# A planner's transfer costs and a second PSUM bank for the last projections, in a fused attention and two-layer-pair kernel

## The chip, the core and the metric

The kernel runs on one core of a Trainium2 chip. The core has five engines that each work through their own instructions in order: TensorE (PE in the profile; its weight loads are a row of their own, PEld), VectorE (DVE), ScalarE (ACT), GpSimd (POOL) and SyncE (SP), which here only issues DMA transfers. The metric is the device time of one execution in microseconds (us); the median of some runs is compared.

## What is computed

```python
def _attn_ref(q, k, v):                       # q, k, v: 8 x 8 heads x 576 x 64
    k_p = k.reshape(B, H, Sp, pool, D).mean(axis=3)      # pool = 8, Sp = 72
    v_p = v.reshape(B, H, Sp, pool, D).mean(axis=3)
    scores = scale * np.matmul(q, k_p.transpose(0, 1, 3, 2))
    attn = np.exp(scores - max); attn = attn / (sum + 1e-09)
    return np.matmul(attn, v_p)
...
def _moe_ref(x, w_in, w_out, g_ln):           # x: 4608 x 512, d_ff 1024
    h = x @ w_in
    solu = h * softmax(h)
    ln = (solu - mu) / np.sqrt(var + 1e-06) * g_ln
    return ln @ w_out
...
def _moe2_ref(x, w_in, w_out):                # d_ff 2048
    h = x @ w_in
    return (h / (1.0 + np.exp(-1.702 * h))) @ w_out
```

The output of each part is the input of the next. The weights come as 8-byte floats and are joined to one number on the chip.

## The kernel before

The kernel has two parts. The **first part** (the first 539 us) computes attention and the first pair of layers and prepares all weights. It works on 36 tiles of 128 tokens. For tile t the steps are, with the names of the program:

- `attention(t)`: load `qt`; PE makes the scores in the PSUM tile `psx`; DVE takes their maximum (`mx`) and subtracts it into `e` (or ACT does it in eight exponentials); ACT takes the exponential; DVE sums (`rs`), ACT and DVE invert the sum; POOL or DVE multiplies; ACT and POOL split the result into two 2-byte halves `st`; SP issues a transposing DMA from `st` to `aT`; PE multiplies `aT` with the values `vst` into the PSUM tile `psv`; ACT and DVE split that into `xT`.
- `Pair.hidden(j)`: PE multiplies `xT` with `w1i` into `psh` (24 products of 512 columns); DVE, ACT and DVE again work on it (`hmx`, `nm`, `he`, `tt`, `mean`, `vs`).
- `Pair.norm()`, for two tiles together: ten small POOL instructions (`q`, `v`, `r`, `a`, `mean`), then for each of the two tiles ACT (`tt`, `zs`), POOL (`zs`) and a transposing DMA to one half of `zT`.
- `Pair.project(half)`, two halves for each of the 18 pairs: 48 products of 256 columns of `zT` with `w1o` into the PSUM tile `psy`; ACT copies `psy` to `y` (two buffers); SP stores `y` to `y_dram`.

Beside that, 16 chunks of the weights of the second pair of layers are loaded (`raw`), joined, combined and split (`w_f`, `hi`, `lo`) by ACT, DVE and POOL, and stored to `w2i_dram` and `w2o_dram`. When the last of them is done, `prepare_second` reloads the seven tiles `w2i` (1 MB each), loads the first block of tokens `y` in four transfers, measures it (`yam`, a diagonal `diag0`, one product into `psx`), scales and splits it into `ys`.

What order these steps take on each engine is set by `Plan.run` while the program is built: a list scheduler. Every step has modelled costs; among the steps that could come next it takes the one with the least of modelled start time and pulled due time, and appends its instruction to its engine's queue. `Op` costs of transfers come from the helper `D` (lines 502 to 507). `take` lets transfers pass one after the other through a modelled resource "dma". The engines then run their queues in that order, whatever the real times are.

PSUM has eight banks here: `psh` twice two, `psx` two, `psy` one, `psv` one. Since `psy` is one tile with one buffer, the second half of a projection may start only when ACT has copied out the first.

The **second part** takes 12 blocks of 384 tokens through the second pair of layers, with the banks `bank_a`, `bank_b` and `bank_d`, in an order that is written out by hand; the change doesn't touch it. Its first instruction on ACT writes the tile `c`, in memory that the first part's `y` buffers held, so it waits for the last store of `y`.

```python
def D(dst, src, turn=False, short=1):
    ...
    n = math.prod(dst.shape) * mybir.dt.size(dst.dtype)
    return Op(("sp",), emit, [dst], [src], {"sp": n / 360 * (1.23 if turn else short)}, turn)
```

Of the kernel before, what the change touches and what calls it, by code (L numbers as in the profile page):

```python
# [8 lines left out]
F32 = mybir.dt.float32  # L9
# [9 lines left out]
P = 128  # L19
B, H, S, D = 8, 8, 576, 64  # L20
# [5 lines left out]
DM = H * D  # L26
# [6 lines left out]
YB = 2 * P  # L33
# [138 lines left out]
class Plan:  # L172
# [30 lines left out]
    def drop(self, *tiles):  # L203
        for t in tiles:
            del self.ring_of[t.name]
# [75 lines left out]
def moe_kernel(ctx: ExitStack, tc: tile.TileContext, qT, kT, vT, w_in, w_out, g_ln, w2_in, w2_out, eye, outT):  # L281
# [135 lines left out]
    with ExitStack() as ph:  # L417
# [7 lines left out]
        psy = ph.enter_context(tc.tile_pool(name="psy", bufs=1, space=PSUM))  # L425
        psv = ph.enter_context(tc.tile_pool(name="psv", bufs=1, space=PSUM))
# [9 lines left out]
        start, drop = plan.start, plan.drop  # L436
# [4 lines left out]
        def there(*ins):  # L441

            return Op(("none",), lambda engine: None, [], ins, {"none": 0})
# [55 lines left out]
        def A(**kw):  # L499
            return op(("act",), "activation", (), kw)  # L500

        def D(dst, src, turn=False, short=1):
            def emit(engine):
                (nc.sync.dma_start_transpose if turn else nc.sync.dma_start)(dst, src)

            n = math.prod(dst.shape) * mybir.dt.size(dst.dtype)
            return Op(("sp",), emit, [dst], [src], {"sp": n / 360 * (1.23 if turn else short)}, turn)

        def T(products):
            def emit(engine):  # L510
                for p in products:
                    nc.tensor.matmul(*p[:3], start=p[3], stop=p[4])  # L512

            outs, ins = {}, {}
            for p in products:
                outs[str(p[0].offset)] = p[0]
                for x in p[1:3]:
                    ins[x.name, x.offset] = x
            c = sum(
                (count(p[2]) * 0.417 + 3 if p[2].dtype == F16 else count(p[2]) * 1.667 + 6)  # L520
                * (0.5 if count(p[1]) == P // 2 else 1)
                for p in products
            )
            return Op(("pe",), emit, list(outs.values()), list(ins.values()), {"pe": c})
# [86 lines left out]
        def raw_load(raw, src, i, n, q):  # L611
            return D(
                raw.rearrange("p q f t -> p q (f t)"),
                src[i * q * P : (i + 1) * q * P, :].bitcast(I32).rearrange("(q p) f -> p q f", p=P),
            )
# [73 lines left out]
        def g_scale():  # L689
            yield D(g_col, g_ln.rearrange("(k p) -> p k", p=P))  # L690
            am, alln = s1("gam"), s1("galln")
            yield absmax_op(am, g_col)
            yield from largest(am, alln, TINY)
            yield from power_scale("_g", alln, 1.0, g_up, g_dn)
            yield V("tensor_scalar_mul", g_col, g_col, g_up)
# [62 lines left out]
        def half(kind, b, j, src, dst):  # L758

            raw = yield New(kv, [P, 2, SP, NPOOL], F32, "half", bufs=3)  # L760
            begun[kind][b] += 1
            yield D(raw.rearrange("p a s o -> p a (s o)"), src[b][:, 2 * j : 2 * j + 2])
            yield from total(G if KV_POOL.get((kind, b)) == j else V, dst[:, 2 * j : 2 * j + 2], raw)
            drop(raw)
# [138 lines left out]
        class Pair:  # L903
# [91 lines left out]
            def project(self, half):  # L995

                yield there(self.zT, *w1o)
                ps = yield New(psy, [P, 2, YB], F32, "psy", "psy")
                for q in range(2):
                    m = 2 * half + q  # L1000
                    yield T(
                        [
                            (
                                ps[:, q],
                                w1o[w][:, k, m * P : (m + 1) * P],
                                self.zT[:, i * K1 + k, :],
                                k == 0 and w == 0 and i == 0,
                                k == K1 - 1 and w == 1,
                            )
                            for k in range(K1)  # L1010
                            for w, i in PASSES
                        ]
                    )
                y = yield New(sb, [P, 2, YB], F32, "y", bufs=2)
                yield A(out=y, in_=ps, func=AF.Copy)
                drop(ps)
                i, o = divmod(self.i * YB, YD)
                yield D(y_dram[i][:, 2 * half : 2 * half + 2, o : o + YB], y)
                drop(y)
# [144 lines left out]
        q_loaded, scored, turned, valued, hid = ([False] * NTILE for _ in range(5))  # L1164
# [315 lines left out]
```

## Time and profile before

| | |
|---|---|
| three runs | 1255.22, 1255.65 and 1250.54 us; median 1255.22 us |
| the profiled execution | 1253.29 us, span from first to last instruction 1251.5 us |
| PE matmul, busy | 1143.5 us, 91% of the span |
| PE weight loads, busy | 989.6 us, 79% |
| ACT, DVE, POOL, busy | 766.5, 730.9, 664.7 us (61, 58, 53%) |
| projections (`psy`) | 1728 matmuls, mean 273 ns as the profile gives them |
| `hidden` (`psh`) | 864 matmuls, mean 389 ns |
| DMA | 152.85 MB, mean 122 GB/s |

The busy shares are means over two parts that differ: in the first all engines and the DMA work together, in the second PE alone is close to full. A matmul's listed duration includes the time that it overlaps the next one, so that 48 projection matmuls take 5.40 us and not 48 times 273 ns. What the engines wait for is read from the timeline and from the list of waits, for one stretch at a time.

### The profile page before, as it was taken

The page shows a single profiled execution, that of the slowest core. Times are in us where ns is not written, and L with a number is a line of the kernel's source. Part 1 is how long each engine was busy: PE and PEld are TensorE (multiplying, and loading weights), DVE is VectorE, ACT ScalarE, POOL GpSimd, SP SyncE. Part 2 cuts the span into 40 slices and gives each one's busy share as a digit, 9 for nine tenths or more (in the row PEclk, how much of TensorE's full clock was granted, in tenths as well). Part 3 has the DMA queues.
Part 4 walks back from the last instruction along what each step waited for, and adds up shares of the span by engine and source line. Part 5 has one row for each costly group of instructions (what it writes and reads, how often), then busy time and mean ns, then how long its engine had stood idle before and what let it go on. Part 6 is the DMA issues. An engine that isn't in the chain of part 4 may idle for free.

```text
span 1251.5 us, 27586 instructions
## 1 busy us (share of the span) xinstructions
PE 1143.5 (91%) x11678; PEld 989.6 (79%) x11678; DVE 730.9 (58%) x1153; ACT 766.5 (61%) x1073; POOL 664.7 (53%) x696
## 2 busy tenths in 40 slices
PE   2778998899999999889999999999999999999998
PEld 2335665576666666789999999999999898999998
DVE  7898877587677843136455454637272737364543
ACT  6998998788789855345445353627263536454552
POOL 5887998687879953424333352525262515243331
PEclk9989999899999999999999999999999999999999
DMA  9979999999989698470101010100011010101000
GB/s 324 302 205 240 269 270 256 248 231 248 256 206 234 164 230 236 109 270 8 46 14 39 14 40 20 33 27 27 27 33 46 7 46 8 46 7 46 14 14 26
DMA packets 246524, 152.85 MB, mean 122 GB/s; under 512 B 163584, under 2 KB 226176, under 8 KB 244096
## 3 DMA queue, kind: packets, MB, share of 16 engines
q1 hardware_dynamic: 246400, 151.09, 45.5%
q8 instruction: 91, 1.49, 0.5%
q14 instruction: 33, 0.27, 0.1%
HBM read 77.66 MB, written 33.55 MB: 89 GB/s over the span
## 4 chain that ended last, share of the span: by engine, by line
PE 30%; POOL 12%; DVE 8%; ACT 8%; issue 5%; DMA 0%; ACTq 0%; POOLq 0%
PE bank_a L1290 18%; PE bank_d L1290 8%; ACT w_g L1325 6%; DVE g L1337 5%; POOL w_g L336 3%; PE bank_b L1290 3%; POOL w_g L335 3%; POOL w_g L333 2%; POOL w_g L334 2%; PE psy L512 2%; ACT g L1334 1%; DVE c L1303 1%; POOL zs L475 1%; DVE w_g L333 0%; ACT c L1300 0%
## 5 line engine op out<-in xcount | busy, mean ns | idle before, releaser
L1290 PEld LDWEIGHTS <-w2i 128*128 128x128 f16 x4032 | 337.4, 98 | 34.3 <-issue 33.7
L1290 PEld LDWEIGHTS <-w2o 128*128 128x128 f16 x4032 | 335.0, 98 | 7.4 <-issue 6.8
L333 POOL TENSOR_TENSOR w_g<-w_g 128x384 f32<-128x384 f32 x36 | 43.6, 1211 | 379.3 <-ACT w_g L1325 379.3
L1290 PE MATMUL bank_a<-ys,w2i 128*128 128x192 f16 x2304 | 215.1, 247 | 27.1 <-ACT c L1300 25.0
L512 PE MATMUL psh<-w1i,xT 128*128 128x512 f16 x864 | 205.8, 389 | 8.9 <-DVE mean L475 8.2
L1290 PE MATMUL bank_a<-g,w2o 128*128 128x192 f16 x2304 | 206.0, 246 | 1.0
L512 PE MATMUL psy<-zT,w1o 128*128 128x256 f16 x1728 | 196.8, 273 | 8.8 <-ACT y L475 8.8
L512 PEld LDWEIGHTS <-w1o 128*128 128x128 f16 x1728 | 167.9, 98 | 35.8 <-issue 10.3
L1337 DVE SCALAR_TENSOR_TENSOR g<-w_g,gu_b,g 128x1152 f16<-128x1152 f32 (+1 forms) x96 | 169.1, 1782 | 24.5 <-ACT g L1334 24.4
L512 PEld LDWEIGHTS <-xT 128*128 128x128 f16 x864 | 84.4, 100 | 103.9 <-issue 13.8
L1300 ACT ACTIVATE c<-bank_a 128x384 f32<-128x384 f32 x192 | 91.7, 484 | 116.4 <-PE bank_a L1290 113.1
L1334 ACT ACTIVATE g<-w_g,gu_b 128x1152 f16<-128x1152 f32 (+1 forms) x96 | 132.9, 1408 | 39.4 <-POOL w_g L336 39.0
L1303 DVE SCALAR_TENSOR_TENSOR c<-bank_d,c 128x384 f32<-128x384 f32 x96 | 53.3, 555 | 134.4 <-ACT c L1300 99.5
L475 POOL TENSOR_TENSOR zs<-tt,zs 128x1024 f16<-128x1024 f32 x36 | 77.4, 2149 | 59.7 <-ACT zs L475 59.5
L1290 PE MATMUL bank_d<-ys,w2i 128*128 128x192 f16 x1152 | 107.5, 249 | 0.3 <-DVE c L1303 0.3
L1290 PE MATMUL bank_d<-g,w2o 128*128 128x192 f16 x1152 | 102.4, 246 | 3.0 <-DVE g L1337 3.0
L1325 ACT ACTIVATE w_g<-c,ch_b 128x1536 f32<-128x1536 f32 x48 | 75.3, 1568 | 36.8 <-DVE c L1303 36.7
L1300 ACT ACTIVATE c<-bank_a,co_b 128x384 f32<-128x384 f32 x47 | 26.9, 573 | 108.6 <-PE bank_a L1290 108.6
L512 PE MATMUL psx<-kbd,qt 128*128 128x144 f32 (+1 forms) x320 | 46.3, 306 | 24.6 <-ACT raw_z L475 12.7
L512 PEld LDWEIGHTS psx<-kbd,qt 128*128 128x128 f32 (+1 forms) x320 | 41.4, 193 | 29.4 <-issue 12.7
L475 POOL TENSOR_TENSOR lo<-w_f,hi 128x512 f16<-128x512 f32 (+1 forms) x46 | 62.2, 1365 | 2.7 <-ACT hi L475 2.3
L475 DVE TENSOR_REDUCE hmx<-psh 128x1 f32<-128x1024 f32 x36 | 43.7, 1214 | 34.1 <-PE psh L512 34.1
(189 smaller groups left out, 1693.1 us busy)
## 6 DMA issues: line engine op xcount, KB each, us to landing
raw<-w_out SPq DMA_DIRECT2D x12, 1024.0 KB, 6.9
raw<-w_in SPq DMA_DIRECT2D x10, 1024.0 KB, 8.0
half<-kT SPq DMA_DIRECT2D x16, 576.0 KB, 5.4
half<-vT SPq DMA_DIRECT2D x16, 576.0 KB, 5.5
qt<-qT SPq DMA_DIRECT2D x36, 256.0 KB, 3.9
y_dram<-y SPq DMA_DIRECT2D x36, 256.0 KB, 2.8
y<-y_dram SPq DMA_DIRECT2D x48, 192.0 KB, 3.2
outT<-c SPq DMA_DIRECT2D x48, 192.0 KB, 1.9
```

Source lines behind the costliest of these rows:

```text
L333: eng.tensor_tensor(out=w[:, 1], in0=q[:, Q12], in1=q[:, Q11], op=ALU.subtract)
L334: eng.tensor_tensor(out=w[:, 2], in0=q[:, Q22], in1=w[:, 1], op=ALU.subtract)
L335: eng.tensor_tensor(out=w[:, 0], in0=q[:, Q22], in1=q[:, Q12], op=ALU.subtract)
L336: eng.tensor_tensor(out=w[:, 3], in0=q[:, Q21], in1=w[:, 2], op=ALU.subtract)
L475: getattr(eng, name)(*args, **kw)
L512: nc.tensor.matmul(*p[:3], start=p[3], stop=p[4])
L1290: nc.tensor.matmul(bank[:, q], self.weight(p, q, kk, w), self.data(p, kk, i), start=(first and q == 0 and kk == 0 and w == 0 and i == 0), ...
L1300: nc.scalar.activation(out=self.c[:, i], in_=bank, func=AF.Copy, scale=self.scale)
L1303: nc.vector.scalar_tensor_tensor(out=self.c[:, i], in0=bank, scalar=self.scale, in1=self.c[:, i], op0=ALU.mult, op1=ALU.add)
L1325: nc.scalar.activation(out=self.w[:, 0:4], in_=self.c, func=AF.Gelu_apprx_sigmoid, scale=self.ch)
L1334: nc.scalar.activation(out=self.g[:, 0, s], in_=self.w[:, s], func=AF.Copy, scale=self.gu)
L1337: nc.vector.scalar_tensor_tensor(out=self.g[:, 1, s], in0=self.w[:, s], scalar=self.gu, in1=self.g[:, 0, s], op0=ALU.mult, op1=ALU.subtract,)
```

## The change

Two edits, both in the first part.

```diff
-        def D(dst, src, turn=False, short=1):
+        def D(dst, src, turn=False):
...
-            return Op(("sp",), emit, [dst], [src], {"sp": n / 360 * (1.23 if turn else short)}, turn)
+            return Op(("sp",), emit, [dst], [src], {"sp": n / (170 if turn else 330)}, turn)
...
             def project(self, half):
...
-                ps = yield New(psy, [P, 2, YB], F32, "psy", "psy")
+                if half and valued[-1]:
+                    flat = yield New(psv, [P, DM], F32, "psv", "psv")
+                    ps = flat.rearrange("p (a t) -> p a t", a=2)
+                else:
+                    flat = ps = yield New(psy, [P, 2, YB], F32, "psy", "psy")
...
-                drop(ps)
+                drop(flat)
```

The first changes the modelled time of every transfer: a plain one of n bytes is counted n/330 ns in place of n/360, and a transposing one n/170 in place of n/293 (360/1.23). For the 512 KB of an `aT` or a `zT` half that is 3.08 us in place of 1.79. No instruction's work changes by that; the planner's order does, on every engine, from the start of the first part to its end. The second lets the second half of a projection go to the bank `psv` once the planner has placed the values' product of the last tile (`valued[-1]`). In the built program that holds for the last four pairs: four of the 36 projection halves go to `psv`.

**Values and hidden layer of a tile.** PE, at tile 32 of 36, before: the end of that tile's product with the values (`psv_5478`), and what follows; `xT_5168` is tile 30.

```order
5021 L512 MATMUL psv_5478<-aT_5263,vst1_120 64x128
5022 L512 LDWEIGHTS vst1_120
5023 L512 MATMUL psv_5478<-aT_5263,vst1_120 64x128
5024 L512 LDWEIGHTS xT_5168
5025 L512 MATMUL psh_5345<-w1i0_115,xT_5168 128x512
```

PE at the same tile, after: `psv_5606` is tile 32's product with the values, and `xT_5623` is made from it.

```order
5201 L512 MATMUL psv_5606<-aT_5528,vst1_120 64x128
5202 L512 LDWEIGHTS vst1_120
5203 L512 MATMUL psv_5606<-aT_5528,vst1_120 64x128
5204 L512 LDWEIGHTS xT_5623
5205 L512 MATMUL psh_5643<-w1i0_115,xT_5623 128x512
```

The hidden product that follows a tile's values was two tiles behind and is now that tile's own.

**ACT at the end of the first part**, before: `he` are the exponential and the square of the last tile (35), `y` the projections' copies, `ys` the first token block, `tt` and `zs` the last pair's two halves.

```order
560 L475 ACTIVATE he_6293,hsm_5880<-psh_6058,nm_6241,h_sc_85 128x1024
561 L475 ACTIVATE he_6293,vs_5882<-tt_6295,mean_5881 128x1024
562 L475 ACTIVATE y_6320<-psy_6222 128x512
563 L475 ACTIVATE ys_6395<-y_6097,y_up_6269 128x1152
564 L475 ACTIVATE ys_6395<-w_y_6286,y_up_6269 128x1536
565 L475 ACTIVATE y_6393<-psy_6335 128x512
566 L475 ACTIVATE tt_6108<-tt_6108,mean_5881,a_6326 128x1024
567 L475 ACTIVATE zs_6406<-tt_6108 128x1024
568 L475 ACTIVATE tt_6295<-tt_6295,mean_5881,a_6326 128x1024
569 L475 ACTIVATE zs_6460<-tt_6295 128x1024
570 L475 ACTIVATE y_6457<-psy_6400 128x512
```

ACT at the same place, after, from the last tile's square (`he`, `vs`) on.

```order
557 L475 ACTIVATE he_6243,vs_5895<-tt_6245,mean_5894 128x1024
558 L475 ACTIVATE y_6306<-psy_6246 128x512
559 L475 ACTIVATE y_6367<-psv_6271 128x512
560 L475 ACTIVATE tt_6108<-tt_6108,mean_5894,a_6278 128x1024
561 L475 ACTIVATE zs_6485<-tt_6108 128x1024
562 L475 ACTIVATE y_6455<-psy_6370 128x512
563 L475 ACTIVATE tt_6245<-tt_6245,mean_5894,a_6278 128x1024
564 L475 ACTIVATE zs_6491<-tt_6245 128x1024
565 L475 ACTIVATE y_6516<-psv_6371 128x512
566 L475 ACTIVATE ys_6523<-y_6400,y_up_6497 128x1152
567 L475 ACTIVATE ys_6523<-w_y_6514,y_up_6497 128x1536
568 L475 ACTIVATE y_6580<-psy_6530 128x512
```

The copies take turns between the two banks; the last pair's two halves (`tt`, `zs`) no longer stand together, a copy stands between them; the token block's `ys` moved behind both.

**SP's queue at the same place**, before: the reloads `w2i`, the token block `y_6097` and the transposes of the last pairs.

```order
234 L504 DMA w2i3_5791<-w2i_dram_69 128x4096
235 L504 DMA_TRANSPOSE zT_6014<-zs_6016 128x16x128
236 L504 DMA w2i6_5794<-w2i_dram_69 128x4096
237 L504 DMA y_6097<-y_dram0_63 128x2x192
238 L504 DMA_TRANSPOSE zT_6014<-zs_6056 128x16x128
239 L504 DMA y_6097<-y_dram0_63 128x2x192 x3
240 L504 DMA y_dram4_67<-y_6135 128x2x256
241 L504 DMA y_dram4_67<-y_6212 128x2x256
242 L504 DMA_TRANSPOSE zT_6224<-zs_6226 128x16x128
```

SP's queue after: `zs_6241` is the second half of the last pair but one, `y_6400` the token block, `zT_6482` the last pair.

```order
239 L504 DMA_TRANSPOSE zT_6233<-zs_6241 128x16x128
240 L504 DMA w2i3_6013<-w2i_dram_69 128x4096
241 L504 DMA w2i6_6016<-w2i_dram_69 128x4096
242 L504 DMA y_6400<-y_dram0_63 128x2x192 x4
243 L504 DMA y_dram5_68<-y_6306 128x2x256
244 L504 DMA y_dram5_68<-y_6367 128x2x256
245 L504 DMA_TRANSPOSE zT_6482<-zs_6485 128x16x128
246 L504 DMA y_dram5_68<-y_6455 128x2x256
247 L504 DMA_TRANSPOSE zT_6482<-zs_6491 128x16x128
```

The token block's load stood ahead of the stores of the 28th and 29th projection halves (`y_6135`, `y_6212`, counted from 0); it now stands ahead of the stores of the 30th and 31st.

## Rows read from the trace of the kernel before

**Rows 1.** Stretches: length, busy and count by engine, clock, DMA share, GB/s

```profile
core 0: us, PE busy (x) PEld busy (x) DVE busy (x) ACT busy (x) POOL busy (x), PEclk, DMA share, GB/s
0.00:136.00 136.00, 88.77 (x596) 54.52 (x597) 116.43 (x215) 117.46 (x200) 102.47 (x128) 0.94 0.96 269
136.00:258.00 122.00, 111.53 (x891) 77.50 (x891) 86.64 (x169) 104.81 (x163) 101.46 (x123) 0.97 1.07 259
258.00:495.00 237.00, 227.36 (x1822) 156.39 (x1817) 158.28 (x287) 183.01 (x286) 183.84 (x240) 1.00 0.93 229
495.00:539.00 44.00, 34.71 (x314) 30.46 (x315) 9.01 (x18) 17.59 (x21) 16.04 (x18) 1.00 0.36 95
540.00:560.00 20.00, 19.59 (x216) 19.02 (x214) 7.84 (x10) 10.49 (x14) 5.04 (x4) 0.91 0.96 380
```

**Rows 2.** Waits of PE from 136 to 258: total, times, longest

```profile
PE psv L512 <- DVE xT L475: 8.3, 3, 5.2
```

**Rows 3.** Timeline around tile 15: start, duration, engine, line, what

```profile
195.77 0.64 PE L512 MATMUL psv<-aT,vst 128*64 128x128 f16 x16
...
211.41 0.58 ACT L475 ACTIVATE xT<-psv 128x512 f16<-128x512 f32 x1
...
216.38 0.64 PE L512 MATMUL psv<-aT,vst 128*64 128x128 f16 x16 [1.99 <-DVE xT L475]
```

**Rows 4.** Waits of PE from 258 to 495

```profile
PE psv L512 <- DMA vst<-vx: 3.5, 2, 1.8
PE psy L512 <- ACT y L475: 3.0, 1, 3.0
```

**Rows 5.** Timeline: scores, their maximum, product with values of tiles 0 and 2

```profile
12.73 2.26 PE L512 MATMUL psx<-kbd,qt 128*128 128x144 f32 x8 [12.73 <-ACT raw_z L475]
...
16.89 0.75 DVE L475 TENSOR_REDUCE mx<-psx 128x8 f32<-128x576 f32 x1
...
30.31 0.75 DVE L475 TENSOR_REDUCE mx<-psx 128x8 f32<-128x576 f32 x1
...
30.90 1.06 PE L512 MATMUL psv<-aT,vst 128*64 128x128 f16 x16 [3.50 <-DMA aT<-st]
...
53.24 0.64 PE L512 MATMUL psv<-aT,vst 128*64 128x128 f16 x16 [1.78 <-DMA aT<-st]
53.81 1.25 PE L512 MATMUL psx<-kbd,qt 128*128 128x144 f32 x8
```

**Rows 6.** Timeline of PE at the first part's end

```profile
490.70 4.05 PE L512 MATMUL psh<-w1i,xT 128*128 128x512 f16 x18
...
495.93 5.40 PE L512 MATMUL psy<-zT,w1o 128*128 128x256 f16 x48
504.35 5.40 PE L512 MATMUL psy<-zT,w1o 128*128 128x256 f16 x48 [3.02 <-ACT y L475]
...
511.95 5.40 PE L512 MATMUL psy<-zT,w1o 128*128 128x256 f16 x48 [1.54 <-ACT y L475]
...
530.25 5.40 PE L512 MATMUL psy<-zT,w1o 128*128 128x256 f16 x48 [0.73 <-ACT y L475]
539.07 1.18 PE L1290 MATMUL bank_a<-ys,w2i 128*128 128x192 f16 x12 [3.42 <-ACT c L1300]
```

**Rows 7.** Timeline of ACT there

```profile
494.16 0.60 ACT L475 ACTIVATE y<-psy 128x512 f32<-128x512 f32 x1 [8.77 <-DMA y_dram<-y]
...
511.80 1.23 ACT L475 ACTIVATE tt<-tt,mean,a 128x1024 f32<-128x1024 f32 x1
513.06 1.06 ACT L475 ACTIVATE zs<-tt 128x1024 f16<-128x1024 f32 x1
```

**Rows 8.** POOL's `zs`: minimum, median, maximum (ns); landing of `zT` (us)

```profile
L475 POOL TENSOR_TENSOR zs<-tt,zs x36: 2114/2132/2475, 93.6 to 516.4; 128x1024 f16<-128x1024 f32 x36
...
DMA to landing us min/median/max: 3.6/5.1/9.6
```

**Rows 9.** The chain that ended last, at the last store

```profile
536.37 2.08 DMA y_dram<-y
```

## The prediction

> **What bounds the kernel now.** First the table by stretches [rows 1]: PE idles 47.2 us up to 136, then 10.5 of 122, 9.6 of 237 and 9.3 of the last 44. From 136 on PE is close to full, and the DMA with it: its share of 1.07 and 0.93 says that transfers overlap each other all the time. So about 29 us of PE's idle time could be won behind 136, and the 47.2 ahead of it stand in a stretch where ACT (117.46) and DVE (116.43 of 136) have hardly room. The second part, from 539.07 [rows 6] to the span's end at 1251.5, is untouched and takes 712.4 us; the profiled execution adds 1.8 to the span. The time after is therefore the moment at which `bank_a` starts, plus 714.2, and only the first part's waits are to be counted.
>
> Second, who is waited for in each stretch. From 136 to 258 the largest wait is `psv` for DVE's `xT`, 8.3 us in three pieces [rows 2]. Around tile 15 [rows 3] the reader sees why: PE was done with `psv` at 196.4 and ACT began `xT` only at 211.41, because its queue has other work ahead of it, in an order made for transfers that come sooner. The next tile's values need that bank and wait. In the same stretch the clock is 0.97 (mean of levels 2.4 and 1.2 GHz), at which 122 us lose 0.03 x 122 = 3.7 us. From 258 to 495 the waits are small and of several kinds [rows 4]. At the end three projections wait for ACT's copies of `psy`, 3.02, 1.54 and 0.73 = 5.3 us, and `bank_a` waits 3.42 for ACT's `c` [rows 6]; the chain that ended last shows the last store of `y` ahead of it, 2.08 us [rows 9].
>
> **The middle, 136 to 258.** The new costs make the planner expect transposes at 170 GB/s. The stretch moved 259 GB/s x 122 us = 31.6 MB. Where no transposes run the queues move 380 at a share of 0.96 [rows 1], so 396 GB/s when full. With 19 transposes of 512 KB and two of 256 KB in the stretch (10.5 MB), the other 21.1 MB take 53 us at 396, and 69 us are left for the 10.5: 153 GB/s, nearer to the new cost than to the old 293. (The Trainium skill, page "DMA: Bandwidth & Descriptors", section "Latency and other measured facts", gives a transposing DMA 261 GB/s where the middle dimension isn't contiguous. By that the transposes were done in 40 us of the 122, the old cost was about right, and the new one holds attention back without need; the slower rival below is what it would lead to.) So the plan should now stop putting `xT` behind work that comes late. At most the 8.3 us and the 3.7 of the clock go, 12.0 us; at the other end none of it goes and a wait like that for the transposed `vst`, 3.5 [rows 4], comes on top. I take -7: the 8.3 us go nearly whole, and little of the clock comes back. Ahead of 136 little is reordered; the queue of ACT ahead of single tiles differs by up to about 7 us both ways, so 0, with bounds of -5 and +5.
>
> **Tiles 18 to 35.** Here the order itself is a cost. Between a tile's scores and its values a chain runs on DVE, ACT, POOL and the DMA, and PE works on other products meanwhile. By the durations of a product, 0.225 for `psh` (4.05 / 18), 0.1125 for `psy` (5.40 / 48) [rows 6], 0.64 for a tile's `psv` [rows 3] and 1.25 for its `psx` [rows 5], the products between the two, counted in the built orders, come to a mean of 36 us over these tiles before, never under 30, and to 21 after. At tile 32 they fall from 36 (72 `psh` 16.2, three halves of `psy` 16.2, the rest `psv` and `psx`) to 11 (24 `psy` 2.7, 24 `psh` 5.4, a double `psv`, a `psx`, a diagonal). At tile 33 they are 10, at 28 and 29 15, at 24 16, at 34 18, at 27 19. PE waits where the chain is longer. From the end of tile 0's scores (12.73 + 2.26 = 14.99) to its values (30.90) it took 15.9 us, 14.0 of them from the maximum on; at tile 2 it took 22.9 from the maximum on [rows 5]. Adding the shortfalls, where a wait at one tile also covers the next one whose scores are already done, gives 4 us in all for a chain of 14, 7 for 16, 13 for 18, 19 for 20 and 35 for 23. Before it is 0 for each.
>
> Besides, the hidden product now stands right behind its own values at tiles 27, 31 and 32, so PE waits there for ACT's and DVE's `xT`: [rows 3] show 0.58 for ACT and a wait of 1.99 of which DVE's half is the end, so about 1.9 each, 5.7 together, of which 1.3 at tile 32 only anticipates tile 33's wait: +4.4. Against that, the 9.6 us that PE idles here before belong to particular places of the old order; I let half go, -4.8. With a chain of 16, the one seen at PE's own wait, nearest to the planner's urgent case at the end: +7.3 + 4.4 - 4.8 = +6.9. Bounds: -5 (the chain hidden wholly: 4.4 less all of the 9.6) and +35 (23 us).
>
> **The tail.** Before, from the end of the last hidden product (490.70 + 4.05 = 494.75, call it zero) to `bank_a` it is 44.3 us: six halves of 5.40 = 32.4, the waits of 5.3, the last gap of 3.42, and some of `bank_a` and the diagonal between. After, the copies of four halves need not be waited for, since `psy` and `psv` take turns: 21.6 us. Then a new wait. The third copy, `y_6455`, needs the `y` buffer of `y_6306`, whose store SP issues behind `w2i3`, `w2i6` and the token block, 2.87 MB or 7.2 us at 396 GB/s; ACT's `y` already waited 8.77 us for such a store before [rows 7]. SP gets there when `zs_6241` can be transposed, by the order one and a half halves in, at about 8, so the buffer is free at 8 + 7.2 + the store's 2.08 [rows 9], 17.3; I take 17.7 for the hand-overs. Behind that copy on ACT stand the last pair's second `tt` and `zs`, and behind these its transpose and the last projection: 17.7 + 0.60 + 1.23 + 1.06 [rows 7] + POOL's 2.13 + the landing of `zT`, 3.6 or more [rows 8] = 26.3, against 21.6 at which PE would be free. From 26.7 the last two halves end at 37.5, and the copy, the store (2.08) and `c` give the same 3.4 us as before: 40.9, so -3.4. Bounds: 35.8 if `zT` is not late (-8.5); 46.3 with the median landing of 5.1 (1.5 more) and the 2.87 MB at the mixed 259 GB/s (3.9 more), +2.0. The clock: a wait of 5 us may lower it to its slow level for some of the last projection, as 0.91 stands behind the gap at 539 [rows 1]; the 24 `bank` products that now stand behind the last half shrink that gap in turn. The two are set against each other, 0.
>
> **Sum.** -7 + 6.9 + 0 - 3.4 = -3.5 on 1253.29: 1249.8, rounded 1249.5. The profile stands 1.9 below the median and inside the three runs (1250.54 to 1255.65), so no correction is made. Same means within 0.5% of the median, what a measurement here can tell from no change: 1248.9 to 1261.5.
>
> **Rivals.**
>
> *Slower: attention becomes what PE waits for.* Held back by costs that are too high for the late stretch (share 0.93, 229 GB/s [rows 1]: less full than the middle), attention runs so close ahead of PE that every delay in the chain is a wait of `psv` for `aT`. It decides from a chain of about 20 us: 19.2 + 4.4 - 4.8 - 7 - 3.4 = +8.4, 1261.7; at 23 it gives 34.5 + 4.4 - 4.8 - 10.4 = +23.7, 1277. For it: tile 2's 22.9 us with queues no fuller than these [rows 5]. Against it: the planner puts an urgent tile's steps ahead on all engines, as the shorter 15.9 of tile 0 shows.
>
> *Better: the waits go and none comes.* The middle gives all 12.0, and between that alone and all of the rest with it (the chain hidden, -5; the tail -3.4) lie -12 to -20.4 with the front at 0: 1233 to 1241. For it: nearly all of PE's idle time behind 136 is of the kind that a truer plan removes. Against it: the short leads at tiles 32 and 33.
>
> *It doesn't do what it says.* The transfers vary far more (landings of `zT` 3.6 to 9.6 us [rows 8]) than any one rate tells, so a wait in the middle goes and one as long comes elsewhere; the tail's gain is eaten by the wait for the buffer of `y`: 1250 to 1258.
>
> **How the numbers follow.** Forecast 0.40, 1243 to 1255, half of it under 1248.9; better 0.20, all under; nothing 0.15, inside 0.5% but for a little; slower 0.25, from 1258 to 1280, a sixth of it still inside. Faster by over 0.5%: 0.40 x 0.5 + 0.20 = 0.40; slower 0.21; the same 0.39. The range leaves out a tenth on either side: below 1237, half of the better case, and above 1268, two fifths of the slower one.
>
> **What would show it right or wrong.** In the profile after: in the middle, `psv` no longer waits for DVE's `xT` and the clock stands at 0.99 or more, or that step is wrong. Between 258 and 495, or wherever tiles 18 to 35 then lie, `psv` waits for the DMA `aT` and `psh` for `xT`, together about 12 us, most at tiles 32 and 33; none says that the chain is shorter than I think, over 20 us that the rival has it. In the tail no `psy` waits for ACT's `y`, one projection waits for the DMA `zT` for about 5 us, ACT's `y` waits for a store of `y_dram`, and `bank_a` starts some 41 us after the last hidden product. From there to the end it must be 712 us again; if not, something is moved that I took for untouched. Wrong altogether would be a gain or a loss that lies ahead of 136.

## The result, and the profile of the changed kernel

The changed kernel is slower: 1268.64 us (median of four runs, 1268.34 to 1272.9) against 1254.78 (median of the four of before beside it), a ratio of 1.0116 with an interval of 1.0096 to 1.0137. The forecast was 1249.5 with a range of 1237 to 1268 and a fifth of a chance for slower. The sign is that of the rival in which attention is held back; the mechanism, as will be seen, is not the one that the rival named.

First the stretches. The columns are those of [rows 1], and the first three stretches are the same; the fourth ends with the last hidden product (494.75 before, now 508.29 + 5.34 = 513.63), the fifth is the tail up to `bank_a`.

```profile
0.00:136.00 136.00, 91.63 (x612) 54.92 (x613) 108.59 (x207) 118.01 (x197) 106.43 (x130) 0.94 0.83 247
136.00:258.00 122.00, 114.77 (x894) 78.33 (x892) 87.19 (x167) 98.53 (x156) 89.51 (x111) 0.99 0.94 227
258.00:495.00 237.00, 211.85 (x1665) 144.70 (x1666) 163.71 (x285) 181.82 (x295) 189.89 (x240) 0.96 0.86 222
495.00:513.60 18.60, 18.60 (x136) 13.12 (x135) 4.21 (x8) 13.49 (x17) 8.82 (x13) 1.00 0.81 253
513.60:555.40 41.80, 33.71 (x292) 29.04 (x290) 12.62 (x18) 13.44 (x16) 13.80 (x17) 0.92 0.64 176
```

Against [rows 1]: PE idles 2.9 us less up to 136 (136 - 91.63 = 44.4 against 47.2) and 3.3 less in the middle (7.2 against 10.5), where the clock is 0.99 instead of 0.97. Then it loses: from 258 to 495 it idles 25.2 us instead of 9.6, and the clock is 0.96 instead of 1.00, which is about 237 x 0.04 = 9.5 us more. The last hidden product ends 18.9 us later. Of that the tail gives back 2.5 (41.75 us to `bank_a` at 555.38 instead of 44.3) and the untouched second part 1.2 (1266.6 - 555.4 = 711.2 instead of 712.4): 18.9 - 2.5 - 1.2 = 15.2, the difference of the spans (15.1) but for rounding.

The last two columns tell as much as PE's. The DMA share fell in every one of the first three stretches, from 0.96, 1.07 and 0.93 to 0.83, 0.94 and 0.86. Up to 495 us it moved 0.136 x 247 + 0.122 x 227 + 0.237 x 222 = 113.9 MB, where before it were 0.136 x 269 + 0.122 x 259 + 0.237 x 229 = 122.5 MB. With fewer transfers under way at once, single transposes mostly came sooner: the landing of `zT` now reads as follows, with a median of 4.0 us for the 5.1 of [rows 8] and the same minimum, though the longest took 12.0 us for 9.6.

```profile
L504 SPq DMA_TRANSPOSE zT<-zs x36: 1318/1721/8460, 96.7 to 539.6; - x36
...
DMA to landing us min/median/max: 3.6/4.0/12.0
```

What came later is what was put off: the loads of the second weights. The line of their `w_out` half, whose last two numbers are the first and the last start, reads so in the kernel before,

```profile
L504 SPq DMA_DIRECT2D raw<-w_out x12: 368/632/1568, 31.0 to 378.0; - x12
```

and so in the changed one, 62 us later at its end:

```profile
L504 SPq DMA_DIRECT2D raw<-w_out x12: 432/622/997, 38.3 to 440.3; - x12
```

What PE waits for between 258 and 500, largest first, has changed in kind against [rows 4]:

```profile
PE psh L512 <- DVE mean L475: 12.1, 5, 5.6
PE psh L512 <- DVE nm L475: 6.5, 2, 3.4
PE psy L512 <- ACT y L475: 4.8, 3, 2.0
PE psh L512 <- ACT xT L475: 2.6, 2, 1.9
```

The hidden products wait for DVE, 18.6 us: `psh` has two buffers, and DVE has not yet read the one that is needed. Before the change that wait was one piece, from 258 to 495:

```profile
PE psh L512 <- DVE mean L475: 0.9, 1, 0.9
```

No wait of `psv` for `aT` is among those after the change at all. The longest piece is 5.62 us; PE's line and DVE's ahead of it are these (start, duration, engine, what; DVE's first):

```profile
342.74 4.61 DVE L475 TENSOR_TENSOR w_f<-w_f 128x256 f32<-128x256 f32 x3 [1.05 <-POOL w_f L475]
347.27 1.21 DVE L475 CUSTOM_DVE_ANT_0 tt<-psh,he 128x1024 f32<-128x1024 f32 x1
348.41 0.08 DVE L475 DVE_READ_ACCUMULATOR2_ANT mean<- 128x1 f32 x1
```

```profile
348.54 5.74 PE L512 MATMUL psh<-w1i,xT 128*128 128x512 f16 x18 [5.62 <-DVE mean L475]
```

Three combinations of the second weights stand in DVE's queue ahead of the hidden layer's `tt`; the first waits 1.05 us for POOL, and the three take 4.6 us. Behind the wait the 18 products took 5.74 us, where 18 took 4.05 [rows 6]: the granted clock was 0.69 there (348.5 to 354.2), the mean of the levels 2.4 and 1.2 GHz. In such places the clock's share of the loss arises.

The tail, PE's lines with a wait and the last ones, and the copy on ACT:

```profile
525.40 5.40 PE L512 MATMUL psy<-zT,w1o 128*128 128x256 f16 x48 [1.28 <-DMA zT<-zs]
...
543.33 6.97 PE L512 MATMUL psy<-zT,w1o 128*128 128x256 f16 x48 [6.67 <-DMA zT<-zs]
550.14 5.40 PE L512 MATMUL psv<-zT,w1o 128*128 128x256 f16 x48
555.38 1.15 PE L1294 MATMUL bank_a<-ys,w2i 128*128 128x192 f16 x12
```

```profile
534.61 0.60 ACT L475 ACTIVATE y<-psy 128x512 f32<-128x512 f32 x1 [7.64 <-DMA y_dram<-y]
```

In the tail no projection waits for a copy any more; the last pair's waits for `zT`, because ACT's copy stood waiting 7.64 us for a `y` buffer, as forecast.

### The profile page after: what moved, and what is told of

Read it like the earlier page. It is cut to its first block, busy times and chain, and to the rows that moved or that the text cites. A ratio compares the mean times of both kernels' runs of the same rounds, so it can differ in the third digit from the quotient of the medians.

```text
span 1266.6 us, 27544 instructions
## 1 busy us (share of the span) xinstructions
PE 1150.5 (91%) x11678; PEld 990.1 (78%) x11678; DVE 736.4 (58%) x1150; ACT 769.8 (61%) x1087; POOL 668.5 (53%) x697
## 4 chain that ended last, share of the span: by engine, by line
PE 43%; POOL 19%; ACT 14%; DVE 13%; issue 9%; DMA 2%; ACTq 0%; SPq 0%; POOLq 0%; DVEq 0%
PE bank_a L1294 17%; PE psh L512 7%; PE psy L512 7%; PE bank_d L1294 7%; ACT w_g L1329 6%; DVE g L1341 6%; POOL w_g L336 3%; POOL w_g L335 3%; POOL w_f L475 3%; POOL w_g L333 2%; PE bank_b L1294 2%; POOL w_g L334 2%; POOL lo L475 1%; ACT raw L475 1%; PE psv L512 1%
## 5 line engine op out<-in xcount | busy, mean ns | idle before, releaser
L512 PE MATMUL psh<-w1i,xT 128*128 128x512 f16 x864 | 209.2, 395 | 36.1 <-DVE mean L475 22.3
L333 POOL TENSOR_TENSOR w_g<-w_g 128x384 f32<-128x384 f32 x36 | 44.4, 1234 | 369.5 <-ACT w_g L1329 345.1
L512 PEld LDWEIGHTS <-w1o 128*128 128x128 f16 x1728 | 170.3, 99 | 44.1 <-issue 10.5
L512 PE MATMUL psy<-zT,w1o 128*128 128x256 f16 x1536 | 180.2, 277 | 15.4 <-DMA zT<-zs 8.0
L1304 ACT ACTIVATE c<-bank_a 128x384 f32<-128x384 f32 x192 | 91.7, 484 | 112.5 <-PE bank_a L1294 111.5
L1329 ACT ACTIVATE w_g<-c,ch_b 128x1536 f32<-128x1536 f32 x48 | 75.2, 1568 | 36.7 <-DVE c L1307 36.7
```

The lines of the kernel that those rows point to most:

```text
L333: eng.tensor_tensor(out=w[:, 1], in0=q[:, Q12], in1=q[:, Q11], op=ALU.subtract)
L1304: nc.scalar.activation(out=self.c[:, i], in_=bank, func=AF.Copy, scale=self.scale)
L1329: nc.scalar.activation(out=self.w[:, 0:4], in_=self.c, func=AF.Gelu_apprx_sigmoid, scale=self.ch)
```

## The experiments

All times are medians of four to ten runs; a ratio is to the kernel before, run beside it on the same chip. In the five sets the kernel before took 1254.2 to 1256.1 us, so times of different sets can be compared to about 2 us.

### Which edit, and which constant

The first four kernels take the change apart. The costs alone:

```diff
-                if half and valued[-1]:
-                    flat = yield New(psv, [P, DM], F32, "psv", "psv")
...
+                ps = yield New(psy, [P, 2, YB], F32, "psy", "psy")
```

> The new transfer costs alone; every projection half goes to psy again. Theory A (the costs lose the time, before the projections' end): the last hidden product ends 17 to 20 us later than in the kernel before (494.75 us), the tail is as long as there (44.3 us), and the run takes 1270 to 1275 us. Rival B (the second bank binds values and projections together and loses it): the last hidden product ends within 5 us of the kernel before, and the run takes 1250 to 1258 us.

Measured: 1271.5 us, 1.0104 (1.0075 to 1.0132). The last hidden product ended at 513.8, as in the changed kernel, and the tail up to `bank_a` behind the last projection (557.2) took 43.4 us, close to the 44.3 of before. Rival B is out.

The second bank alone, `"sp": n / (360 / 1.23 if turn else 360)`:

> The second bank alone, with the old transfer costs. Theory A: the order up to the last tile's values stays, so the last hidden product ends at about 495 us; the tail is 2 to 4 us shorter than 44.3 us; 1250 to 1253 us. Rival B: slower than the kernel before by 10 us or more.

Measured: 1246.7 us, 0.9907 (0.9879 to 0.9936). The bank is a gain, larger than expected. In the profiled execution, at 1249.5 the slowest of its four, the tail took 36.7 us (499.75 to 536.43) in place of 44.3, with one wait of 2.86 for `zT`, while the last hidden product ended 5 us later in an order that is the same up to the last values. How much of the 0.9 per cent lies behind the last hidden product is not settled by that one execution.

Only transposes dear, and only copies dear, each with the bank:

```diff
-            return Op(("sp",), emit, [dst], [src], {"sp": n / (170 if turn else 330)}, turn)
+            return Op(("sp",), emit, [dst], [src], {"sp": n / (170 if turn else 360)}, turn)
```

> As the changed kernel, but plain transfers counted at 360 as before and only transposes at 170. Theory A1 (the dear transposes lose the time, since they hold attention back without need): 1265 to 1273 us, waits of psh for DVE in the late tiles as in the changed kernel. Theory A2 (any other set of costs gives another order that loses or wins by chance): anything between 1245 and 1275, and its waits stand at other places than in the changed kernel.

```diff
-            return Op(("sp",), emit, [dst], [src], {"sp": n / (170 if turn else 330)}, turn)
+            return Op(("sp",), emit, [dst], [src], {"sp": n / (360 / 1.23 if turn else 330)}, turn)
```

> As the changed kernel, but transposes counted at 293 as before and only plain transfers at 330. Theory A1: 1249 to 1256 us, since the transposes' cost is the old one. Theory A2: anything between 1245 and 1275.

Measured: 1260.2 us, 1.0034 (1.0010 to 1.0058) with transposes at 170, and 1240.4 us, 0.9866 (0.9828 to 0.9904) with copies alone at 330. Both came out below what was expected of A1, but 20 us apart in its direction: the transposes' cost is the lever. With 330 for copies it is worth 1268.6 - 1240.4 = 28 us, with 360 it is worth 1260.2 - 1246.7 = 13.5. The copies' cost has no sign of its own: 330 in place of 360 gains 6.3 us with transposes at 293 and loses 8.4 at 170.

### How the time goes with the transposes' cost

The same line with other rates in place of 170:

> As the changed kernel, transposes counted at 261 GB/s. Theory A1 (the time grows with the transposes' modelled cost): a little above the 1240 us of 293, 1240 to 1248. Theory A2: no order in the three times at 293, 261 and 215.

> As the changed kernel, transposes counted at 215 GB/s. Theory A1: between the times of 261 and 170, 1248 to 1260 us. Theory A2: no order.

> As the changed kernel, transposes counted at 360 GB/s, cheaper than before the change. Theory A1, if the time only grows with the cost: 1235 to 1242 us. If 293 is near what a transpose takes: some us above the 1240 of 293, with waits of psv for late transposes in the middle. Theory A2: no order.

> The changed kernel with transposes at 172 GB/s in place of 170, 1 per cent cheaper. If the time follows from the cost: 1264 to 1271 us. If any small change of the costs gives another order whose time is a matter of chance: differs from 1268.6 by over 6 us either way. It also tells how far a single constant's result may be read.

> The changed kernel with transposes at 150 GB/s. Theory W: the last weights are measured behind the 31st hidden product as in the changed kernel, so 1265 to 1280 us. If it is chance: anything from 1240 to 1275 us.

| rate of transposes (copies 330) | median us | ratio and interval |
|---|---|---|
| 360 | 1255.2 | 1.0013 (0.9996 to 1.0030) |
| 293 | 1240.4 | 0.9866 (0.9828 to 0.9904) |
| 261 | 1246.0 | 0.9936 (0.9913 to 0.9960) |
| 215 | 1237.0 | 0.9865 (0.9843 to 0.9888) |
| 172 | 1257.7 | 1.0027 (1.0009 to 1.0044) |
| 170 | 1268.6 | 1.0116 (1.0096 to 1.0137) |
| 150 | 1279.7 | 1.0220 (1.0185 to 1.0255) |

The three kernels from 293 to 215 beat the kernel before, and the time rises on both sides. Inside this valley 261 stands 6 and 9 us above its neighbours, so its floor has no shape that could be read. 261 came as A1 had it, and 360 as the sentence on 293 had it, though 15 us above 1240 and not some; A1 as a plain rule (dearer is slower) missed 215, which came out fastest where 1248 to 1260 was expected. 150 lies in W's range and outside that of chance. And 1 per cent of the constant, 170 to 172, moved the time by 11 us, as chance had it: every cost gives another order, and one order's luck is worth nearly as much as the whole change lost (13.9 us) and two fifths of the 28. So no single kernel here proves a cause; what follows rests on pairs. At 360 PE waits for transposes that come later than planned, from 136 to 500:

```profile
PE psv L512 <- DMA vst<-vx: 7.8, 3, 4.9
PE psx L512 <- issue: 5.5, 1, 5.5
PE psy L512 <- DMA zT<-zs: 2.3, 1, 2.3
PE psv L512 <- DMA aT<-st: 2.2, 1, 2.2
```

12.3 us of these are waits for transposes; the kernel of 1240 us has 6.2 there, all for `vst`. So too cheap a cost brings more of such waits, but they are under half of the 15 us: the last hidden product ends 6.9 us later than at 293 (497.1 against 490.3), and the tail up to `bank_a` takes 47.3 us instead of 39.0, with two waits for `zT` of 5.04 and 4.79. 215 and 293 (1237.0 and 1240.4) beat both kernels; they differ from each other by less than two neighbouring constants do.

### The weights' place

The loads that were put off suggested a theory W: the second weights, pushed behind attention, hold up the queues among the last tiles. First the changed kernel with the weights due earlier:

```diff
-STEP_W2 = 19000
+STEP_W2 = 17000
```

> The changed kernel with its transfer costs (170 and 330), only the second weights' chunks are due every 17 us in place of 19, so that the last two are measured behind the 27th hidden product, as before the change, and not behind the 31st. Theory W (the loss is the weights' preparation, pushed behind attention by the dear transposes, which then holds up DVE, ACT and POOL among the last twelve tiles): most of the 28 us between 1240 and 1268 come back, 1242 to 1254 us, and the last chunk lands by 410 us. Rival H (the dear transposes lose by themselves, by the order of values and hidden products): 1262 to 1272 us.

Measured: 1266.8 us, 1.0110 (1.0083 to 1.0136). The last chunk landed at 408 instead of 449, as meant, and nothing was won. From 258 to 500 the hidden products waited for DVE as long as ever:

```profile
PE psh L512 <- DVE mean L475: 20.7, 7, 7.2
PE psy L512 <- ACT y L475: 2.5, 3, 1.1
PE psv L512 <- DMA aT<-st: 2.4, 2, 1.3
```

Its DMA moved 238, 236 and 228 GB/s in the three stretches, 115.2 MB up to 495, where the changed kernel moved 113.9: the weights came earlier and the bytes hardly rose, so other transfers must have come later (which ones was not looked up). Theory W, taken alone, falls. The reverse, the kernel of 1240 us with `STEP_W2 = 23000`:

> Transposes at 293 and copies at 330, the kernel of 1240 us, with the second weights' chunks due every 23 us in place of 19: the last is measured behind the 29th hidden product and not the 26th. Theory W: slower than 1240 by 8 to 20 us, 1248 to 1260, with psh waiting for DVE among the last twelve tiles as in the changed kernel. Rival H: 1237 to 1245 us.

Measured: 1255.5 us, 1.0020 (1.0002 to 1.0039), 15 us lost, as W had it, but not in W's way: between 258 and 500 no `psh` waited for DVE's `mean`; the tail became longer (47.7 us from the last hidden product to the end of the last projection, 39.2 in the kernel that it was made from), with waits of 6.89 and 2.95 for `zT`. It moved 263, 230 and 225 GB/s, 117.2 MB.

Last, the three combinations that stood on DVE ahead of `tt`:

```diff
-                    return VG("tensor_tensor", out=w[:, slot], in0=w[:, a], in1=w[:, b], op=how)
+                    return G("tensor_tensor", out=w[:, slot], in0=w[:, a], in1=w[:, b], op=how)
```

> The changed kernel with the weights' combinations w_f on POOL alone; five of 64 were on DVE before, three of them (4.6 us) just ahead of the tt that PE waited 5.6 us for at 348. If these are the loss: 1255 to 1262 us and no wait of psh for DVE over 3 us. If they are a symptom of queues that are full late: 1263 to 1275 us, with the wait moved elsewhere.

Measured: 1268.6 us, 1.0098 (1.0064 to 1.0131). The wait was spread over other places (258 to 495):

```profile
PE psh L512 <- DVE mean L475: 8.5, 3, 4.2
PE psy L512 <- ACT y L475: 6.4, 4, 4.8
PE psh L512 <- DVE nm L475: 2.9, 1, 2.9
PE psx L512 <- DMA qt<-qT: 2.2, 1, 2.2
```

The pair on DVE and PE shown above is a symptom: neither earlier weights nor an emptier DVE won the time back. That work that has been put off then stands elsewhere, in queues that are worked off in order, fits both kernels, but it is argued and not shown.

### Late, or long

The cost of a transfer enters the planner twice: what it writes is there after that time, and the modelled resource "dma" (with it SP's queue, for a transpose) is taken for that time. The next four kernels separate the two. "Late" leaves the data's time at 170 or 150 and takes the resource only for the time at 293; "long" is the reverse.

```diff
-            self.free["dma"] = end = begin + op.cost["sp"]
-            self.free["sp"] = max(t + 625, end - 920) if op.turn else t + 520
+            end = begin + op.cost["sp"]
+            self.free["dma"] = gone = begin + op.cost["sp"] * (170 * 1.23 / 360 if op.turn else 1)
+            self.free["sp"] = max(t + 625, gone - 920) if op.turn else t + 520
```

> As the changed kernel, with one difference in the planner: what a transpose writes is still modelled as there after the time at 170 GB/s, but the modelled transfer resource and SP's queue are given free after the time at 293. Theory A1a (170 is a waiting time of a full queue, counted as time in which nothing else is moved; that holds transfers back and loses): most of the loss behind the transposes' cost (1240 with 293 and 330, 1268.6 with 170 and 330) comes back, 1240 to 1252 us, the DMA share from 136 to 258 back at 1.0 or more. Theory A1b (the later modelled landing itself moves values and hidden products): 1260 to 1272 us. Theory A2 (any other order wins or loses by chance): anything between.

> As the kernel with transposes at 150 GB/s (1279.7 us), but the modelled transfer resource and SP's queue are taken for the time at 293 only; the data is modelled as there after the time at 150. Theory O (the modelled occupation loses the time): 1238 to 1256 us. Theory L (the later landing loses it): 1268 to 1285 us.

The reverse, at 170 and at 150 (the factor then stands in the line of `end`):

> The other half at 170: the data is modelled as there after the time at 293, but the transfer resource and SP's queue are taken for the time at 170. Theory O: 1258 to 1275 us, the last chunks' loads after 430 us, a DMA share from 136 to 258 under 0.97. Theory L: 1238 to 1256 us.

> The same at 150. Theory O: 1265 to 1290 us. Theory L: 1238 to 1256 us.

| | at 170 | at 150 |
|---|---|---|
| both (the changed kernel's way) | 1268.6, 1.0116 (1.0096 to 1.0137) | 1279.7, 1.0220 (1.0185 to 1.0255) |
| late, not long | 1249.3, 0.9966 (0.9945 to 0.9988) | 1250.1, 0.9971 (0.9949 to 0.9993) |
| long, not late | 1265.4, 1.0084 (1.0055 to 1.0113) | 1293.3, 1.0298 (1.0256 to 1.0339) |

Together with the kernel in which both times are those at 293 (1240.4 us) this makes four pairs for each half. The longer occupation costs 25.0 and 52.9 us where the landing is early, and 19.4 and 29.6 where it is late: four differences of one sign, each beyond the 11 us of luck. The later landing costs 8.9 and 9.7 us where the occupation is short, and 3.2 and -13.6 where it is long: either sign, hardly beyond luck. So the modelled occupation loses the time; whether by the resource "dma" or by SP's modelled queue, which is taken with it, was not separated. Two details were missed: long at 150 came out 3 us above O's range, and the DMA share of long at 170 in the middle was 0.97 and not under it (late at 170 had 1.09, as A1a had it); its last weights' load was issued at 442.0. The stretches of "late" at 150 and of "long" at 150 show where (columns as above):

```profile
0.00:136.00 136.00, 93.37 (x621) 56.66 (x622) 114.12 (x218) 119.31 (x202) 104.35 (x129) 0.94 0.97 263
136.00:258.00 122.00, 114.02 (x914) 79.12 (x913) 90.49 (x168) 104.71 (x166) 103.07 (x127) 0.97 1.06 258
258.00:495.00 237.00, 225.61 (x1775) 155.31 (x1773) 148.67 (x281) 184.47 (x284) 187.24 (x241) 0.99 0.94 233
```

```profile
0.00:136.00 136.00, 93.68 (x606) 55.79 (x607) 106.09 (x204) 116.31 (x194) 100.58 (x126) 0.92 0.79 232
136.00:258.00 122.00, 114.76 (x909) 80.34 (x907) 82.33 (x151) 92.09 (x146) 96.57 (x124) 1.00 0.89 221
258.00:495.00 237.00, 203.59 (x1542) 137.72 (x1541) 152.85 (x289) 181.90 (x293) 177.18 (x219) 0.92 0.83 211
```

Up to 258 PE does about as much in both, 207.4 and 208.4 us (1535 and 1515 matmuls); the DMA share is 0.97 and 1.06 against 0.79 and 0.89. The bill comes behind 258: 225.61 against 203.59 us of PE's work in 237, at a clock of 0.99 against 0.92. The bytes moved up to 495 us, worked out from the last column as above, set the kernels with the second bank in one row:

| MB up to 495 us | kernels | us |
|---|---|---|
| 121.7 to 123.5 | 293, 261, 215, late at 170 and 150, bank alone | 1237 to 1250 |
| 116.4 to 117.2 | 360, 172, transposes alone at 170, weights later | 1255 to 1260 |
| 112.5 to 115.2 | changed, long at 170, weights earlier, combinations on POOL | 1265 to 1269 |
| 108.5 and 111.0 | long at 150, 150 | 1293, 1280 |

This goes with the time, but in part it follows from it: a kernel that is behind has moved less by 495 us. That the occupation causes the loss is shown only for the pairs in which it alone was changed.

One figure is known before any run and sorts the kernels as well. While a kernel is built, `take` carries a modelled time for every engine; the modelled end of the last projection on PE is no time of the chip, only what the planner itself expects:

| modelled end of the last projection, us | kernels | measured us |
|---|---|---|
| 490 to 503 | before, bank alone, 293, 261, 215, 360, late at 170 and 150, weights later | 1237 to 1256 |
| 514 | transposes alone at 170 | 1260 |
| 529 to 540 | changed, costs alone, 172, long at 170, weights earlier, combinations on POOL | 1258 to 1272 |
| 563 and 569 | 150, long at 150 | 1280, 1293 |

The changed kernel's plan ends at 535.6 us, 42.9 behind the 492.7 of the plan before; on the chip its last projection ended 19.9 us later (555.54 against 535.65). Within the first row the figure tells nothing of the 19 us between fastest and slowest.

## Why the prediction was wrong

**The middle: the term came, and the working ahead of it is where the failure begins.** -7 was forecast, -3.3 of idle time and -2.4 of clock came, and `psv` no longer waits there for `xT`. But the working ahead of it took 259 GB/s, gave the copies 396 and left the transposes 153, "nearer to the new cost than to the old 293". That charges to the transposes everything that a full queue costs all who stand in it. The planner itself adds 1.275 us ahead of every transpose and 0.95 up to its reader (`take`, `LAG`), so the new cost makes 1.275 + 3.08 + 0.95 = 5.3 us from issue to use, about the median landing of 5.1 in the busy queue [rows 8], and the old one 4.0. The minimum of 3.6 us for 512 KB [rows 8] stood against it, and it stayed 3.6 in the changed kernel; a `vst` of 256 KB lands there in 3.1 at least,

```profile
DMA to landing us min/median/max: 3.1/3.4/5.5
```

so the second 256 KB add some 0.5 us, and most of the 3.6 doesn't grow with the bytes: an estimate from two minima, but far from the 3.08 us that the new cost makes of 512 KB alone. The Trainium skill, page "DMA: Bandwidth & Descriptors", section "Latency and other measured facts", gives a transposing DMA 261 GB/s where the middle dimension isn't contiguous. No run here measures that rate by itself. A planner that was given it took 1246.0 us, 22.6 less than with 170, so it was the better guide here than the 153 that was worked out, though 293 and 215 took less still.

**What the plan then believes was not worked out.** Up to 495 us the kernel before issued 68 transposes of 512 KB and 8 of 256 KB, 37.7 MB. By the new costs they take 37.7 / 0.170 = 222 us and the other 84.7 MB of the 122.5 take 84.7 / 0.330 = 257: 479 of 495 us, a resource that is full to the brim. By the old ones it is 129 + 235 = 364 us. The planner's own model agrees: up to its last hidden product its transfers fill 0.95 of the time, and 0.80 in the plan before. The prediction asked what each wait would do and not what a planner does that thinks its scarcest resource is full: it holds back whatever is not due yet, and here the loads of the second weights came 62 us later at their end.

**Tiles 18 to 35: the step that failed.** +6.9 was forecast, the largest part of it from `psv` waiting for `aT` at short leads such as those of tiles 32 and 33; +25.1 came, by another wait. `psv` waited for `aT` not at all: the chain ran short enough, with landings that were quicker than before. `psh` waited 2.6 us for `xT`, where 5.7 were counted. What came was +15.6 of idle time and 9.5 of clock. Most of the idle time is `psh` waiting for DVE, 18.6 us, a wait that no part of the prediction priced: before the change it is 0.9 us in one piece in this stretch. The late and long kernels show that the planner's modelled occupation makes the loss; how it becomes just these waits is shown for one place (three put-off combinations ahead of `tt` on DVE) and stays open for the rest. The clock's loss behind waits was thought of in the tail alone and not counted here.

**The slower rival** had sign and size (1258 to 1280, measured 1268.6), and "held back by costs that are too high" is what the runs show. Its mechanism, attention so close ahead of PE that `psv` waits for `aT`, is not: that wait is 0. That its time came near was luck.

**The tail: right in its waits, near in size in part by luck.** 40.9 us forecast, 41.75 measured; ACT's copy stood for the store (7.64), the last pair's projection for `zT` (6.67, and 1.28 for the pair ahead), no copy was waited for. Two errors cancelled. The last half ended 41.9 us after the last hidden product and not 37.5: ACT's copy began at 21.0 and not 17.7, and the projection behind the wait ran partly at the slow clock (0.76 granted, 6.97 us instead of 5.40). Against that, the gap ahead of `bank_a` went entirely instead of staying at 3.4.

**Ahead of 136** 0 was forecast, -2.9 came, inside its bounds. The second part took its 712 us again, less 1.2. Read so, the terms come to -2.9 - 5.7 + 25.1 - 2.5 - 1.2 = +12.8 of the 15.1 us; the other 2.3 lie within the rounding of the clock column (0.005 of 495 us is 2.5).

## What to carry to other kernels

A landing time read from a busy queue holds the waiting; put into a planner as the time in which a transfer fills the resource, it makes the planner keep apart transfers that the chip carried together. The shortest landings are no better as a constant: 256 KB more in some 0.5 us would be 524 GB/s (an estimate from two minima), and at 360 the gain was gone already. Rates between, 215 to 293, did best here. Add up the modelled occupation over the stretch: a sum that comes near the stretch itself (479 of 495 us here) says that the constants will steer everything else. Read the planner's own end time too, before anything runs: it was 42.9 us later for the changed kernel. And where a list scheduler is rebuilt by a constant, measure neighbouring constants before a result is read: 1 per cent was worth 11 us here.

## What the runs showed of the hardware

The transposing DMA of 512 KB into `zT` landed in 3.6 to 3.7 us at the least in all 18 kernels, whether the DMA share in the middle was 1.09 or 0.89; between the kernel before and the changed one the median went from 5.1 to 4.0, the longest from 9.6 to 12.0.

Scattered waits of PE cost some two fifths to three fifths as much again in clock. With 25.2 us of idle time in 237 the granted clock read 0.96 (9.5 us), with 33.4 (long at 150) it read 0.92 (19 us), and with 9.6 it read 1.00 [rows 1].

The five combinations of 128 x 256 that the changed kernel ran on DVE, beside a busy POOL, took 0.83 to 2.23 us each, while the three that the kernel before ran on DVE took 0.41 to 0.83 (the first of them with POOL idle):

```profile
L475 DVE TENSOR_TENSOR w_f<-w_f x5: 827/1490/2229, 284.8 to 346.5; 128x256 f32<-128x256 f32 x5
```

```profile
L475 DVE TENSOR_TENSOR w_f<-w_f x3: 412/425/832, 442.1 to 443.0; 128x256 f32<-128x256 f32 x3
```

What makes the difference was not tried.
